# Key sums of two tiles at a time, a block of query projections moved, and another order at the start

## The chip, the cores and the metric

The program runs on one core of one Trainium2 chip. The engines that matter here are TensorE (PE: matmuls, and PEld: its weight loads), VectorE (DVE), ScalarE (ACT), GpSimd (POOL), and SyncE (SP), which issues most DMA transfers. Each engine takes its own instructions in order; semaphores hold an instruction until what it needs has been produced. The metric is the device time of one execution in microseconds (us), as the median of some runs.

## The reference

Linear attention, then a gated network, then a soft mixture of experts, in float32:

```python
def phi(x):                                   # q, k: (4 batches, 8 heads, 576, 64)
    proj = einsum('bhsd,df->bhsf', x, w_phi)  # 128 features
    proj = proj - max(abs(proj), axis=-1)
    return concatenate([exp(proj), exp(-proj)], axis=-1)
q_p, k_p = phi(q), phi(k)
kv = einsum('bhsf,bhsd->bhfd', k_p, v)
z  = sum(k_p, axis=2)
x  = einsum('bhsf,bhfd->bhsd', q_p, kv) / (einsum('bhsf,bhf->bhs', q_p, z) + 1e-6)
...
x = rms_norm(x) ; x = (silu(x @ w_gate) * (x @ w_val)) @ w_out     # 2304 tokens, 512 -> 1536 -> 512
...
d = softmax over tokens of (x @ phi) ; slots = d.T @ x ; experts ; c = softmax over slots
```

## The kernel before, in words

There are three stages. The first makes, for each of the four batches, the sums kv and z over its 576 keys, and the attention output of the first 384 query tokens (block 0). The second runs the gated network over six blocks of 384 tokens, with the queries of the later blocks turned into attention outputs in between. The third runs the experts. The change touches the first stage alone.

**Keys.** The 2304 keys are 18 tiles of 128. For each tile, class K does: `project` (L503, tile name P): 8 heads by 64-row matmuls, in two halves of four heads, the halves alternating; the two halves use different rows of the array and run side by side. `shift` for each half: on VectorE the largest absolute value (L507, `largest`) and the difference (L511, `less`). `exps` for each half: two exponentials on ScalarE (L524, L525) into a tile kp. `kv`: first `kv_of` for both halves (L548, kacc from kp and vt: each head's values as 64-column weights, two heads side by side), then `z_of` for both halves (L557, kacc from kp and small: a block of ones as 32-column weights, four heads side by side). They accumulate in PSUM over a batch. A batch is four and a half tiles, so tiles 4 and 13 are cut in two parts, and there are 20 parts. Where a batch ends, `Evac` copies its sums out (L570, L572) and three `fillers` transpose them (L585, kvt) and copy them into place (L594, L596). Each matmul in float32 leaves two records in the trace.

The loop over tiles i emits P and shift of tile i + 2, then the sums of tile i, then the exponentials of tile i + 2. P has two PSUM buffers, one for each half, so P of the next tile waits until `less` has read both halves of the one before. A pool named "misc" of three PSUM buffers is shared by the transposes of the sums and everything for block 0.

**Block 0.** Class Rows handles four pairs of heads. For each pair c and each of three 128-token pieces: `project` (L389, P from qraw; then L392 and L393 on VectorE), two half tiles later `turn` (L404 transposes, L406 exponentials), and once per pair `attend` (L449, o; L452 to L454). `scale` squares and normalizes rows (L465, L466 to L469), `out` transposes them back (L476, L477). Which half tile (2i or 2i + 1) each of these is emitted at is written out by hand in the list TURNED0: starts of the projections of the four pairs, then the four attend steps, then scale and out.

**Weights.** In the same stage nine pieces of the second stage's weights are loaded (L142) and converted on ScalarE and VectorE (L146, L148, L156, L158, L121, L124), one step each half tile from half tile 7.

**Order.** The instructions are emitted in this order, and a planner then orders each engine's instructions by its own estimate of when each is ready, with emission order as the priority. `placed(f, engines)` adds an edge so that the instructions that f emits on an engine stay behind the last one emitted there, and in their own order. WARM matmuls on zeros (L609) keep PE at work before the first keys have landed.

Of the kernel before, what the change touches and what calls it, by code (L numbers as in the profile page):

```python
# [7 lines left out]
F32 = mybir.dt.float32  # L8
F32R = mybir.dt.float32r
U32 = mybir.dt.uint32  # L10
AF = mybir.ActivationFunctionType
ALU = mybir.AluOpType
# [4 lines left out]
NB, NH, SEQ, HD, DF = 4, 8, 576, 64, 128  # L17
# [11 lines left out]
KCONV, MCONV = (3, 2), (2, 2)  # L29
NX = 4  # L30
CFIRST = 7
WARM = 3
NLEFT = 2
ELEFT = 4
CTURN = 4
# [1 line left out]
PADDED = [3, 3, 3, 6, 8, 8, 18, 13, 18]  # L37
PLAST = [2, 2, 2, 6, 9, 9, 15, 12, 15]
ADDED = [-6, -2, -1, 0, 2, 1, 2, 3, 4, 6, 6, 9, 8, 12, 10, 11, 13, 14, 13, 14, 16, 17, 18, 18, 21, 20, 24, 25, 28, 30]
TURNED0 = [2, 8, 14, 20, 12, 15, 20, 26, 28, 33]  # L40
TURNED1 = [0, 3, 10, 17, 6, 13, 20, 26, 27, 29, 31]


# [24 lines left out]
def tile_kernel(ctx: ExitStack, tc: tile.TileContext, q2T, qT, kT, v, wbd, wg, wv, wo, rmsg, phi, w1, w2, consts, out):  # L68
# [4 lines left out]
    def placed(f, *engines):  # L73

        traced = nc.cur_bb.bb.instructions
        start = len(traced)
        f()
        traced = nc.cur_bb.bb.instructions
        for engine in engines:
            last = next((i for i in reversed(traced[:start]) if i.engine == engine), None)  # L80
            for i in traced[start:]:
                if i.engine == engine:
                    if last is not None:
                        tc.add_manual_dep(i, last.name, nosync, reason="placed")
                    last = i
# [351 lines left out]
    class Rows(Turned):  # L437


        def attend(self, c):  # L440
            if c == 0:
                self.y = self.sp.tile([128, TPB, 4, 2, HD], F32, tag="y", name="y", bufs=1)
            e = [self.e.pop(2 * c), self.e.pop(2 * c + 1)]
            o = self.psum("o", [128, TPB, 2, HD + 1])
            for i in range(TPB):
                for b, r0, r1 in batch_parts(self.blk * TPB + i):
                    for hh in range(2):
                        for s in range(2):
                            PE.matmul(out=o[r0:r1, i, hh], lhsT=e[hh][:, s, 128 * i + r0:128 * i + r1],  # L449
                                      rhs=kvt[b][:, 2 * c + hh, s], start=s == 0, stop=s == 1, skip_group_check=True)  # L450
            rd = self.sp.tile([128, TPB, 2, 1], F32, tag="rd", name="rd", bufs=2)
            DVE.tensor_scalar(out=rd, in0=o[:, :, :, HD:HD + 1], scalar1=1e-6, scalar2=None, op0=ALU.add)  # L452
            DVE.reciprocal(out=rd, in_=rd)
            DVE.tensor_tensor(out=self.y[:, :, c], in0=o[:, :, :, 0:HD], in1=rd.to_broadcast([128, TPB, 2, HD]), op=ALU.mult)  # L454
            for b, t0, t1 in block_parts(self.blk):
                if c == 3 and self.blk * BLK + t1 == (b + 1) * SEQ and b + 2 < NB:
                    kvt[b + 2] = kvp.tile([128, NH, 2, HD + 1], F32, tag="kv", name=f"kv{b + 2}", bufs=2)
                    SP.dma_start(out=kvt[b + 2].rearrange("p h s d -> p (h s d)"), in_=kv_d[b + 2])

        def scale(self):  # L460
            sq = self.sp.tile([128, 2, 2, BLK], F32, tag="e", name="sq", bufs=self.bufs["e"]).rearrange("p a b t -> p (a b t)")
            ms = self.sp.tile([128, TPB], F32, tag="ms", name="ms", bufs=1)
            rows = [self.y[:, i].rearrange("p c h d -> p (c h d)") for i in range(TPB)]
            for i in range(TPB):
                ACT.activation(out=sq[:, DM * i:DM * i + DM], in_=rows[i], func=AF.Square, accum_out=ms[:, i:i + 1])  # L465
            DVE.tensor_scalar(out=ms, in0=ms, scalar1=1.0 / DM, scalar2=1e-6, op0=ALU.mult, op1=ALU.add)  # L466
            rsqrt(self.sp, ms)
            for i in range(TPB):
                DVE.tensor_scalar(out=rows[i], in0=rows[i], scalar1=ms[:, i:i + 1], scalar2=None, op0=ALU.mult)  # L469

        def out(self):
            xraw[self.blk] = xp.tile([128, 4, BLK], F32, tag="xraw", name="xraw", bufs=1)
            for c in range(4):
                tp = self.psum("yT", [128, TPB, 128])
                for i in range(TPB):
                    PE.transpose(out=tp[:, i], in_=self.y[:, i, c].rearrange("p h d -> p (h d)"), identity=ident)  # L476
                ACT.activation(out=xraw[self.blk][:, c].rearrange("p (i t) -> p i t", i=TPB), in_=tp, func=AF.Copy, scale=rms_sb[:, c:c + 1])  # L477

    with ExitStack() as pk:
        kx = pool(pk, "kx")  # L480
        sp = pool(pk, "spk")
        psk = pool(pk, "psk", PSUM)
        acc = {}

        class Front:

# [30 lines left out]
        class K(Front):  # L517
# [2 lines left out]
                SP.dma_start(out=self.vt, in_=v[self.i].rearrange("p (h d) -> p h d", h=NH))  # L520

            def exps(self, hf):
                kp = sp.tile([128, 4, 2, DF], F32, tag="kp", name="kp", bufs=6)
                ACT.activation(out=kp[:, :, 0], in_=self.pr[hf], func=AF.Exp)  # L524
                ACT.activation(out=kp[:, :, 1], in_=self.pr[hf], func=AF.Exp, scale=-1.0)  # L525
                self.e[hf] = kp

            def kv(self, part):

                for f in (self.kv_of, self.z_of):  # L530
                    for hf in range(2):
                        f(hf, part)

            def ends(self, part):
                b, r0, r1 = part
# [86 lines left out]
        for k in ks[0:2]:  # L622
            k.project()
            for hf in range(2):
                k.shift(hf)
                k.exps(hf)
        fillers = []
        q0 = Rows(sp, psk, 0, {"misc": 3, "raw": 2, "pr": 3, "e": 2})
# [3 lines left out]
        for i in range(TILES):  # L632
            k, kn = ks[i], ks[i + 2] if i + 2 < TILES else None
            if i + 4 < TILES:
                ks[i + 4].load()
            if i + 2 < TILES:
                ks[i + 2].load_v()
            parts = batch_parts(i)
            b = parts[0][0]
            ends = i * 128 + parts[0][2] == (b + 1) * SEQ  # L640

            def finish():
                ev = Evac(b)
                fillers.extend([lambda n=n: ev.turn(n) for n in range(3)])

            if len(parts) > 1:
                k.kv(parts[0])
                finish()
            if kn:
                kn.project()  # L650
                kn.shift(0)
                kn.shift(1)
            k.kv(parts[-1])
            for hf in range(2):
                if kn:
                    kn.exps(hf)
                n = 2 * i + hf - CFIRST
                if (n + 5) % 3 == 0 and 0 <= n + 5 and (n + 5) // 3 < NPRE:
                    placed(lambda: conv_load(sp, KCONV, sp), SP.engine)
                if n >= 0:  # L660
                    if n % 3:
                        conv_join()
                    else:
                        conv_parts()
                        conv_scale()
                if fillers:
                    fillers.pop(0)()
                for f in qsteps[2 * i + hf]:
                    f()
            if ends and len(parts) == 1:  # L670
                finish()
# [528 lines left out]
```

## Time and profile before

| | us |
|---|---|
| median of 3 runs | 704.33 (703.95 to 706.42) |
| profiled execution: time | 705.7 |
| profiled execution: span from first to last instruction | 703.9 |
| TensorE busy, share of the span | 689.4, 98% |
| VectorE busy | 468.5, 67% |
| ScalarE busy | 329.1, 47% |

The profile is of one execution. Busy time of an engine is the time in which one of its instructions ran; a matmul's end is modelled, so a busy PE need not be at its peak rate. "Idle before" names what ended an engine's idle time before an instruction. The granted clock of TensorE is a share of 2.4 GHz.

### The profile page before, as it was taken

What the parts mean: (1) busy time and instruction counts of PE and PEld (TensorE: products, weight loads), DVE (VectorE), ACT (ScalarE), POOL (GpSimd) and SP (SyncE); (2) the same over time, 40 slices, a digit from 0 to 9 for tenths busy, and PEclk for the clock granted to TensorE, in tenths of its full rate; (3) what the DMA queues carried; (4) which work ended last, traced back from release to release, by engine and by line L of the source; (5) the groups of instructions that cost most, each with busy time, mean ns of one, the idle gap of its engine ahead of it and who ended that gap; (6) DMA issues with size and microseconds to landing.
All of it is one profiled execution on the core that took longest, in us unless ns stands there. A gap on an engine that the chain in (4) does not pass through costs nothing.

```text
span 703.9 us, 11807 instructions
## 1 busy us (share of the span) xinstructions
PE 689.4 (98%) x4653; PEld 571.3 (81%) x4653; DVE 468.5 (67%) x915; ACT 329.1 (47%) x687; POOL 147.2 (21%) x74
## 2 busy tenths in 40 slices
PE   7999999999999999999999999999999999999995
PEld 4667766988889898998989989899897999898443
DVE  4798995888875596765857669776585753423313
ACT  4878885687745443344432554425443232112103
POOL 0000000000003355133651326523364200000100
PEclk9999999999999999999999999999999999999997
DMA  6755535434211001010000100001000085577898
GB/s 224 280 170 192 195 107 181 143 120 160 79 40 33 3 24 40 0 57 12 24 9 1 57 13 23 9 0 57 1 1 8 1 305 234 190 284 256 323 367 291
DMA packets 25143, 79.42 MB, mean 113 GB/s; under 512 B 2688, under 2 KB 13376, under 8 KB 18688
## 3 DMA queue, kind: packets, MB, share of 16 engines
q1 hardware_dynamic: 24720, 77.52, 31.4%
q10 hardware_dynamic: 368, 1.15, 0.5%
q8 instruction: 36, 0.59, 0.3%
q14 instruction: 19, 0.16, 0.1%
HBM read 71.99 MB, written 6.67 MB: 112 GB/s over the span
## 4 chain that ended last, share of the span: by engine, by line
PE 96%; DMA 1%; ACT 1%; DVE 1%; issue 0%; SPq 0%; ACTq 0%
PE pg L928 22%; PE pv L928 22%; PE acc L953 7%; PE acc L954 7%; PE acc L955 7%; PE kacc L548 5%; PE num L223 4%; PE P L503 3%; PE kacc L557 3%; PE y L1088 2%; PE y L1072 2%; PE o L449 2%; PE P L389 1%; DMA wraw<-in_wo_dram 1%; PE x2tp L738 1%; PE qP L315 1%
## 5 line engine op out<-in xcount | busy, mean ns | idle before, releaser
L928 PE MATMUL pv<-xnh,wv 128*128 128x384 f32 x576 | 117.1, 343 | 0.0
L928 PE MATMUL pg<-xnh,wg 128*128 128x384 f32 x576 | 115.1, 342 | 0.3 <-ACT xnh L121 0.3
L318 POOL PARTITION_ALL_REDUCE qe<-qe x32 | 51.9, 1634 | 297.1 <-ACT qe L317 287.9
L928 PEld LDWEIGHTS pg<-xnh,wg 128*128 128x128 f32 x576 | 102.5, 188 | 5.8 <-ACT xnh L121 0.7
L928 PEld LDWEIGHTS pv<-xnh,wv 128*128 128x128 f32 x576 | 101.7, 188 | 1.5 <-issue 1.3
L349 POOL PARTITION_ALL_REDUCE qe<-qe x32 | 82.7, 2631 | 85.8 <-DVE qe L348 56.3
L121 ACT CAST hh<-t 128x384 fp32r<-128x384 f32 x72 | 36.7, 509 | 115.2 <-PE acc L954 77.6
L953 PE MATMUL acc<-wo,hh 128*128 128x512 f32 x216 | 87.2, 404 | 0.0
L954 PE MATMUL acc<-wo,hh 128*128 128x512 f32 x216 | 86.1, 399 | 0.0
L955 PE MATMUL acc<-wo,hl 128*128 128x512 f32 x216 | 85.3, 395 | 0.0
L124 DVE TENSOR_TENSOR hl<-t,hh 128x384 fp32r<-128x384 f32 x72 | 40.1, 557 | 63.3 <-ACT hh L121 63.2
L936 DVE SCALAR_TENSOR_TENSOR t<-t,pg 128x384 f32<-128x384 f32 x72 | 39.8, 553 | 57.9 <-ACT t L935 57.7
L935 ACT ACTIVATE t<-pg 128x384 f32<-128x384 f32 x72 | 35.1, 487 | 73.1 <-PE pg L928 72.7
L928 PE MATMUL pg<-xnl,wg 128*128 128x384 f32 x288 | 65.0, 342 | 0.0
L928 PE MATMUL pv<-xnl,wv 128*128 128x384 f32 x288 | 62.4, 339 | 0.0
L940 DVE TENSOR_TENSOR t<-t,pv 128x384 f32<-128x384 f32 x72 | 39.6, 549 | 24.6 <-PE pv L928 23.6
L928 PEld LDWEIGHTS pg<-xnl,wg 128*128 128x128 f32 x288 | 51.9, 188 | 1.6 <-DVE xnl L124 0.9
L928 PEld LDWEIGHTS pv<-xnl,wv 128*128 128x128 f32 x288 | 51.7, 188 | 0.0
L955 PEld LDWEIGHTS acc<-wo,hl 128*128 128x128 f32 x216 | 40.6, 188 | 10.2 <-DVE hl L124 0.3
L953 PEld LDWEIGHTS acc<-wo,hh 128*128 128x128 f32 x216 | 40.8, 189 | 7.3 <-issue 0.3
L954 PEld LDWEIGHTS acc<-wo,hh 128*128 128x128 f32 x216 | 40.6, 188 | 6.3
L548 PE MATMUL kacc<-kp,vt 128*64 128x256 f32 (+1 forms) x320 | 41.2, 393 | 2.3 <-ACT kp L525 2.3
(207 smaller groups left out, 1051.7 us busy)
## 6 DMA issues: line engine op xcount, KB each, us to landing
eu<-in_w_dram SPq DMA_DIRECT2D x32, 1024.0 KB, 6.6
wraw<-in_wg_dram SPq DMA_DIRECT2D x6, 1024.0 KB, 4.9
wraw<-in_wv_dram SPq DMA_DIRECT2D x6, 1024.0 KB, 5.6
wraw<-in_wo_dram SPq DMA_DIRECT2D x6, 1024.0 KB, 5.5
qraw<-in_qT_dram SPq DMA_DIRECT2D x32, 192.0 KB, 2.4
vt<-in_v_dram SPq DMA_DIRECT2D x18, 256.0 KB, 3.2
out_dram<-ob SPq DMA_DIRECT2D x18, 256.0 KB, 3.0
raw<-in_kT_dram SPq DMA_DIRECT2D x17, 256.0 KB, 2.9
```

The source lines that it names most:

```text
L121: ACT.copy(out=hi, in_=src)
L124: (lo_eng or POOL).tensor_tensor(out=lo, in0=src, in1=hi.bitcast(F32), op=ALU.subtract)
L318: POOL.partition_all_reduce(e[:, 0], e[:, 1], channels=128, reduce_op=bass_isa.ReduceOp.absmax)
L349: POOL.partition_all_reduce(e[hh][:, 1], u, channels=128, reduce_op=bass_isa.ReduceOp.add)
L548: PE.matmul(out=kva[o0:o0 + 64, hh // 2], lhsT=self.vt[r0:r1, h], rhs=kp[r0:r1, hh].rearrange("p s f -> p (s f)"), start=first and hh < 2, ...
L928: PE.matmul(out=p, lhsT=w[:, a, c], rhs=x, start=n == 0, stop=n == 11)
L935: ACT.activation(out=t, in_=g, func=AF.Tanh, scale=0.5)
L936: DVE.scalar_tensor_tensor(out=t, in0=t, scalar=1.0, in1=g, op0=ALU.add, op1=ALU.mult)
L940: DVE.tensor_tensor(out=t, in0=t, in1=wide("v", m, xs), op=ALU.mult)
L953: PE.matmul(out=acc[i], lhsT=hh[:, s], rhs=w[:, 0], start=m == 0, stop=False)
L954: PE.matmul(out=acc[i], lhsT=hh[:, s], rhs=w[:, 1], start=False, stop=False)
L955: PE.matmul(out=acc[i], lhsT=hl[:, s], rhs=w[:, 0], start=False, stop=m == MF - 1)
```

## The change

The sums z of a part are no longer issued behind its key-value matmuls: the part is put in a list `zs`, and the list is worked off when it holds two parts or the part ends its batch. kp gets 8 buffers instead of 6. The number of warm-up matmuls rises from 3 to 4. For the first two tiles VectorE's instructions are placed in emission order (largest, less of one half, then of the other; the same for tile 1), and the projections of tiles 2, 3 and 4 are placed on PE. In TURNED0 the projections of pair 1 start at half tile 11 (8 before), those of pair 2 at 15 (14), and the attend steps of pairs 1 and 2 are at 17 and 21 (15 and 20). Block 0's attention output is kept in the tile xraw from the start, and transposed and written back in place, so its own tile y goes.

```diff
-WARM = 3
+WARM = 4
-TURNED0 = [2, 8, 14, 20, 12, 15, 20, 26, 28, 33]
+TURNED0 = [2, 11, 15, 20, 12, 17, 21, 26, 28, 33]
...
         def attend(self, c):
             if c == 0:
-                self.y = self.sp.tile([128, TPB, 4, 2, HD], F32, tag="y", name="y", bufs=1)
+                xraw[self.blk] = xp.tile([128, 4, BLK], F32, tag="xraw", name="xraw", bufs=1)
...
-            DVE.tensor_tensor(out=self.y[:, :, c], in0=o[:, :, :, 0:HD], ...)
+            DVE.tensor_tensor(out=xraw[self.blk][:, c].rearrange("p (i h d) -> p i h d", i=TPB, h=2), in0=o[:, :, :, 0:HD], ...)
...
-            rows = [self.y[:, i].rearrange("p c h d -> p (c h d)") for i in range(TPB)]
+            rows = [xraw[self.blk][:, :, 128 * i:128 * i + 128] for i in range(TPB)]
...
         def out(self):
-            xraw[self.blk] = xp.tile([128, 4, BLK], F32, tag="xraw", name="xraw", bufs=1)
...
-                    PE.transpose(out=tp[:, i], in_=self.y[:, i, c].rearrange("p h d -> p (h d)"), identity=ident)
+                    PE.transpose(out=tp[:, i], in_=xraw[self.blk][:, c, 128 * i:128 * i + 128], identity=ident)
...
-        acc = {}
+        acc, zs = {}, []
...
-                kp = sp.tile([128, 4, 2, DF], F32, tag="kp", name="kp", bufs=6)
+                kp = sp.tile([128, 4, 2, DF], F32, tag="kp", name="kp", bufs=8)
...
             def kv(self, part):
-                for f in (self.kv_of, self.z_of):
-                    for hf in range(2):
-                        f(hf, part)
+                for hf in range(2):
+                    self.kv_of(hf, part)
+                zs.append((self, part))
+                if len(zs) == 2 or self.ends(part)[1]:
+                    for k, p in zs:
+                        for hf in range(2):
+                            k.z_of(hf, p)
+                    zs.clear()
...
         for k in ks[0:2]:
             k.project()
             for hf in range(2):
-                k.shift(hf)
+                placed(lambda: k.shift(hf), DVE.engine)
                 k.exps(hf)
...
             if kn:
-                kn.project()
+                placed(kn.project, *[PE.engine] * (i < 3))
                 kn.shift(0)
                 kn.shift(1)
```

## Rows read from the trace of the kernel before

**Rows 1.** Page, busy time by engine: us, share of the span, instructions.

```profile
PE 689.4 (98%) x4653; PEld 571.3 (81%) x4653; DVE 468.5 (67%) x915; ACT 329.1 (47%) x687; POOL 147.2 (21%) x74
```

**Rows 2.** Windows by stage: length, busy time by engine, PE clock, DMA share, GB/s.

```profile
13.20:118.05 104.85, 103.20 (x1092) 68.50 (x1091) 89.22 (x155) 80.86 (x151) 0.00 (x0) 1.00 0.52 178
118.05:643.00 524.95, 524.81 (x2987) 469.61 (x2988) 354.06 (x699) 230.69 (x497) 144.26 (x68) 1.00 0.20 71
```

**Rows 3.** Windows in the beginning, same columns.

```profile
7.22:9.48 2.26, 0.00 (x1) 0.00 (x0) 2.26 (x5) 1.20 (x3) 0.00 (x0) 1.00 0.96 347
9.70:13.00 3.30, 3.30 (x12) 0.96 (x8) 1.54 (x3) 2.96 (x6) 0.00 (x0) 0.50 0.80 300
```

**Rows 4.** Timeline of the beginning: start, duration, engine, line, instruction, idle before.

```profile
1.18 2.77 PE L609 MATMUL idle<-still 128*32 128x256 f32 x6 [1.18 <-DVE small L606]
...
4.25 2.97 PE L503 MATMUL P<-wbd_f,raw 64*128 64x128 f32 x32 [0.30 <-DMA raw<-in_kT_dram]
...
6.36 1.29 DVE L507 TENSOR_REDUCE mx<-P 128x4 f32<-128x512 f32 x2 [1.70 <-PE P L503]
...
8.28 0.63 ACT L524 ACTIVATE kp<-pr 128x512 f32<-128x512 f32 x1 [3.62 <-DVE pr L511]
...
9.48 1.88 PE L548 MATMUL kacc<-kp,vt 128*64 128x256 f32 x8 [2.26 <-ACT kp L525]
...
13.21 1.17 PE L503 MATMUL P<-wbd_f,raw 64*128 64x128 f32 x16
...
14.41 1.29 DVE L507 TENSOR_REDUCE mx<-P 128x4 f32<-128x512 f32 x2 [3.17 <-PE P L503]
...
17.33 1.49 PE L503 MATMUL P<-wbd_f,raw 64*128 64x128 f32 x16
...
20.76 1.13 PE L389 MATMUL P<-wbd_f,qraw 128*128 128x256 f32 x4
```

**Rows 5.** Chain of work that ended last, tiles 15 and 16: start, time until the next.

```profile
95.99 0.22 PE kacc L557 x5
...
104.43 1.09 PE P L503 x16
105.52 1.88 PE kacc L548 x16
107.40 1.00 PE kacc L557 x16
```

**Rows 6.** Timeline around the wait in mid-stage.

```profile
36.99 1.19 ACT L146 ACTIVATE wt<-wraw 128x1024 f32<-128x1024 f32 x1 [0.74 <-DMA wraw<-in_wo_dram]
...
40.84 0.70 PE L389 MATMUL P<-wbd_f,qraw 128*128 128x256 f32 x2 [1.33 <-ACT kv L596]
```

**Rows 7.** Timeline: VectorE's last differences and PE's next projections.

```profile
70.12 1.28 DVE L511 TENSOR_TENSOR pr<-P,mx 128x512 f32<-128x512 f32 x2
...
71.88 1.16 PE L503 MATMUL P<-wbd_f,raw 64*128 64x128 f32 x16
...
82.75 1.28 DVE L511 TENSOR_TENSOR pr<-P,mx 128x512 f32<-128x512 f32 x2
...
84.97 1.16 PE L503 MATMUL P<-wbd_f,raw 64*128 64x128 f32 x16
```

**Rows 8.** Window over tiles 10 to 17, columns as before.

```profile
61.64:108.33 46.69, 46.69 (x510) 31.50 (x509) 45.30 (x82) 38.11 (x73) 0.00 (x0) 1.00 0.44 142
```

**Rows 9.** Timeline: two engines writing parts of one tile.

```profile
71.89 0.63 ACT L596 COPY kv<-kvt 128x256 f32<-128x256 f32 x2
...
72.44 0.75 DVE L594 COPY kv<-kvt 128x256 f32<-128x256 f32 x2
```

**Rows 10.** Lines by form, 0 to 118 us: busy us, mean ns, idle before.

```profile
L511 DVE TENSOR_TENSOR pr<-P,mx 128x512 f32<-128x512 f32 x36 | 23.2, 684 | 0.0
...
L392 DVE TENSOR_REDUCE qmx<-P 128x2 f32<-128x256 f32 x12 | 5.1, 422 | 1.3 <-PE P L389 1.2
...
L469 DVE TENSOR_SCALAR y<-y,ms 128x512 f32<-128x512 f32 x3 | 1.3, 482 | 0.0
```

More of the change, by code (lines that the diff above doesn't have):

```diff
@@ L453, in attend @@
             DVE.reciprocal(out=rd, in_=rd)
-            DVE.tensor_tensor(out=self.y[:, :, c], in0=o[:, :, :, 0:HD], in1=rd.to_broadcast([128, TPB, 2, HD]), op=ALU.mult)
+            DVE.tensor_tensor(out=xraw[self.blk][:, c].rearrange("p (i h d) -> p i h d", i=TPB, h=2), in0=o[:, :, :, 0:HD], in1=rd.to_broadcast([128, TPB, 2, HD]), op=ALU.mult)
             for b, t0, t1 in block_parts(self.blk):
@@ L462, in scale @@
             ms = self.sp.tile([128, TPB], F32, tag="ms", name="ms", bufs=1)
-            rows = [self.y[:, i].rearrange("p c h d -> p (c h d)") for i in range(TPB)]
+            rows = [xraw[self.blk][:, :, 128 * i:128 * i + 128] for i in range(TPB)]
             for i in range(TPB):
-                ACT.activation(out=sq[:, DM * i:DM * i + DM], in_=rows[i], func=AF.Square, accum_out=ms[:, i:i + 1])
+                ACT.activation(out=sq[:, DM * i:DM * i + DM].rearrange("p (c t) -> p c t", c=4), in_=rows[i], func=AF.Square, accum_out=ms[:, i:i + 1])
             DVE.tensor_scalar(out=ms, in0=ms, scalar1=1.0 / DM, scalar2=1e-6, op0=ALU.mult, op1=ALU.add)
```

## Prediction, made before the changed kernel was run

> **What bounds the kernel now.** I read the page's busy times first: TensorE (PE) is busy 98% of the span [rows 1]. Then the windows by stage: the first stage, after its beginning, runs from 13.20 to 118.05 us with PE busy 103.20 of 104.85 us, and the second is closed to within 0.2 us [rows 2]. So after the beginning the program is one string of PE work, and the change can gain only what PE idles, what it runs at a lower clock, or what it spends between kinds of matmul. Nothing in the diff touches the second or third stage; what the first stage gains moves the rest forward whole.
>
> Next the beginning. In the timeline, look at who waits for whom: PE projects tiles 0 and 1 (P, from 4.25), VectorE (DVE) takes maxima and differences from 6.36, ScalarE (ACT) starts exponentials at 8.28, and PE waits 2.26 us, to 9.48, for the first of them [rows 4]. The windows show PE empty from 7.22 to 9.48 and then a granted clock of 0.50, that is 1.2 of 2.4 GHz, over 9.70 to 13.00 [rows 3]. P of tile 2 comes only at 13.21, though its PSUM buffers were free when VectorE went idle at 11.24 (14.41 less 3.17) [rows 4].
>
> Last the two places where PE could lose time later: the one wait in mid-stage, 1.33 us before 40.84 for a copy on ACT [rows 6], and how closely VectorE follows PE. VectorE is busy 45.30 of 46.69 us between 61.64 and 108.33 [rows 8], with PE never waiting there: two engines near their limit side by side.
>
> **The change part by part.**
>
> *Feature sums two by two.* A tile costs PE a projection of 1.09 us, a key-value group of 1.88 and a sum group (z) of 1.00 [rows 5]. In z four matmuls run side by side; one round takes 0.22 (the row of the last five), and 16 records are four rounds, 0.86 (at 0.215). The other 0.14 is the change of array shape, paid on entering and leaving z. There are 20 parts of tiles (18 tiles, two cut by a batch's end). With sums held until two are there or the batch ends, each batch of five parts makes three z groups, not five: 12, not 20, so 8 times 0.14 = 1.1 us. Where tile 15 is followed by tile 16 with no projection between, two key-value groups also join; eight rounds of 0.215 are 1.72 of 1.88, so 0.16 more. Bounds: nothing, if the planner parts the joined groups again; 0.4 each if all idle time of the weight loads around a z went too. I take 0.14: it is counted from the group itself. One merge falls into the beginning (below); the other seven with the joined key-value groups give **1.1**. The two extra kp buffers only hold what waits; v tiles are released by the key-value matmuls as before, so SP's queue is not held longer.
>
> *The beginning.* The fourth warm-up matmul is two more records at the pace of the first six, at most 2.77 / 6 = 0.46 each [rows 4]: they end near 4.6 to 4.8, and P starts near 4.7, not 4.25. As the later rounds of P then run at the higher rate, its end for tile 0 moves less: VectorE starts near 6.6 (0.27 later; bounds 0, if the load lands later still, and 0.86). VectorE's eight instructions took 6.36 to 11.24, 0.61 each. Now they go in pairs, maximum then difference of one half, so the first half is ready after two, not three: 6.6 + 1.2, and ACT starts near 7.9 (8.28 before); PE follows 1.2 after ACT's start, as now [rows 4], near 9.1, and with P of tile 1 ending near 7.5 (7.22 before) it idles 1.6 us, not 2.26. VectorE is through with tile 1 near 11.5; P of tile 2 can start then, not at 13.21, if the planner puts it there: the new chain on PE keeps P after what precedes it in the program and its two halves interleaved. Tile 3's P took 1.42 to the next group (1.09 interleaved), 0.33 lost [rows 4, 5]. Adding up what PE must do from there: P2 to 12.7, key-values of tile 1 to 14.6, both z groups to 16.45, P3 to 17.55. Before, the same work was done at 20.76 [rows 4]. That is 3.2 us if the clock stays up. If it falls again, PE is at half speed to about 13 and the same sum ends at 18.55: 2.2 us. Which? After 2.26 us of idling it fell [rows 3]; after the 1.33 us before 40.84 [rows 6] the next groups are at full pace. 1.6 us is nearer to the second, but no row decides it. I take **2.7**; bounds 0.5 (only the VectorE order helps) and 3.4.
>
> *Three half tiles later.* At half tile 8 and 9 two projections of block 0 were due among the transposes of batch 0's key-value sums. All share three "misc" PSUM buffers; ACT, late because its weight scaling waited 0.74 us for a load, copied them out late, and the projection stood 1.33 us at the head of PE's queue [rows 6], with the next tile's P behind it. The projections now come at half tiles 11 to 13. The work is the same: per projection one matmul, two transposes and VectorE's reduction (0.42) [rows 10] and subtraction. Pair 2 moves one half tile, the attention steps of pairs 1 and 2 two and one. SP's load of pair 3 is issued three half tiles later, 7 half tiles ahead of its use. With only three transposes left, the misc buffers suffice: gain **1.33** (bounds 0, if the same wait comes later, and 1.33).
>
> *y in place of its own tile.* Rows of a token tile are now four runs of 128, not 512 in one run. The three scalings took 482 ns each [rows 10], on the way to the transposes. If strides cost, the nearest row above is a two-input instruction of the same 512 elements, 684: at most 0.6 us in all. I take 0: four instructions of 128 have the same elements, and key-value and sum groups of tiles 16 and 17 can stand in PE's queue meanwhile. The Trainium skill, "VectorE: DVE Perf Modes", section What auto-detection actually checks, ties the double rate to an even outermost dimension, which four runs keep; by it the term is 0 too, and no row here shows a strided one. ScalarE writes back into the tile that PE still transposes from; two engines do write parts of one tile at once here (ACT 71.89 to 72.52, VectorE from 72.44) [rows 9], so parts are tracked apart: 0.
>
> *What is late next.* A tile that gives up its z has 1.0 us less PE work before the next P, and that P needs VectorE's last difference. For tile 12's P there were 0.48 us to spare (71.40 to 71.88), for tile 14's 0.94 (84.03 to 84.97) [rows 7]. Both follow tiles that defer (9 and 11), and the moved attention step puts about 0.9 us of VectorE work before the first. So 0.3 to 1.1 us of waiting at the first, about 0.1 at the second, and up to 0.6 each at two others: 0.3 to 2.2; I take **1.0** lost, as the receiving tile gives nothing back while PE is the bound.
>
> Sum: 2.7 + 1.33 + 1.1 - 1.0 = 4.1 us. The profiled execution took 705.7 us with a span of 703.9; the sum makes it 701.6 and 699.8. It was 1.4 above the median of the runs, 704.33, which I forecast at **700.2**.
>
> **The rivals.**
> *The beginning gives little.* PE takes instructions in order, and the planner orders by its own times; it put single key-value and z matmuls ahead of P2 before. If it still does, only VectorE's new order helps, 0.5 of 2.7: 702.4. For it: the chain binds P to what precedes it, not what follows to P. Against: with paired halves everything is ready earlier.
> *The wait moves.* The moved projections meet attention steps and transposes for the same misc buffers where VectorE is 97% busy [rows 8]; then the 1.33 comes back, and VectorE's waits may reach their upper bound: 701.5 to 702.7. Against: PE was busy without a break from 61.64 to 108.33, through the same kind of steps [rows 8].
> *Pairs of sums save nothing.* If the 0.14 belongs to the matmuls themselves, or the planner parts them: 1.26 less gain, 701.5. Against it: 0.22 for a round of z.
> *Slower.* One mechanism: VectorE, not PE, sets the pace in every deferring tile. Then PE waits there up to the 1.0 us it no longer spends, and the sum work, put into the next tile, comes on top. With eight such tiles, and gains of 5.1 before waits, it decides from 0.64 us a tile; at 1.0 the loss is 8.0 and the time 707.2. Against it: the tiles in [rows 7] are the tightest of the deferring ones, and they have half a microsecond and more of the 1.0.
>
> **How the numbers follow.** A difference under 0.5%, 3.5 us, is about what cannot be told from no change. Forecast (698.9 to 701.3) 0.50; the wait moves 0.20; beginning gives little 0.15; sums save nothing 0.10; slower 0.05. Faster than 700.8 are most of the first case and the lower ends of the next three: 0.56. Slower than 707.9 lies only beyond the last case: 0.03. The rest, 0.41, is within. From 698.7 to 702.6 hold the first four but for tails; that leaves under 2 in 10 out.
>
> **What would show it.** Right: 12 z groups in the timeline, of 32 records and 1.86 us where joined; P of tile 2 near 11.6; no 0.50 clock, or a shorter spell; no PE wait for ACT's copy; second stage starting near 114.0, not 118.05. Wrong: new PE waits for VectorE before P in tiles 9 and 11, key-value matmuls standing ahead of P2, a wait for a misc buffer between 50 and 80 us, or PE waiting for the scaled rows before the last transposes.

## The result, and the profile after

The changed kernel takes **708.95 us** (median of 4 runs, 708.60 to 709.48), the kernel before on the same chip 704.53 (4 runs, 703.95 to 706.42). The ratio is 1.0059 with a 95% interval of 1.0038 to 1.0079: slower by some 4 us, where 700.2 was forecast. In some of the experiments below a part of the runs took 10 us or more longer than the others, for a reason that no run shows; ratios are of the shorter runs.

The profiled execution took 708.62 us with a span of 706.7 (before: 705.7 and 703.9), so the traces account for 2.9 of the 4.4 us; the profiled execution of before was one of its longer ones. First the page's busy times, as in [rows 1]:

```profile
PE 693.6 (98%) x4655; PEld 573.9 (81%) x4655; DVE 468.6 (66%) x915; ACT 329.4 (47%) x687; POOL 147.2 (21%) x74
```

PE has 4.2 us more busy time for two more records, those of the fourth warm-up matmul. The windows say where, with the columns of [rows 2]:

```profile
13.20:118.05 104.85, 104.83 (x1062) 69.07 (x1061) 88.14 (x152) 79.17 (x145) 0.00 (x0) 1.00 0.52 178
7.22:9.48 2.26, 0.47 (x10) 0.28 (x8) 2.19 (x5) 1.15 (x2) 0.00 (x0) 1.00 0.97 322
9.70:13.00 3.30, 3.30 (x27) 1.39 (x23) 2.35 (x4) 2.88 (x6) 0.00 (x0) 1.00 0.88 318
61.64:108.33 46.69, 46.69 (x482) 32.66 (x480) 42.75 (x74) 36.98 (x72) 0.00 (x0) 1.00 0.40 131
120.31:645.26 524.95, 524.80 (x2987) 469.45 (x2988) 354.06 (x699) 230.75 (x497) 144.25 (x68) 1.00 0.20 71
```

Several things that I had forecast are here. From 9.70 to 13.00 the granted clock is 1.00 where [rows 3] had 0.50, with 27 records done for 12. From 13.20 on PE is never idle: the wait of [rows 6] is gone, and the list of waits has for the rest of the first stage only this:

```profile
PE pg L932 <- ACT xnh L121: 0.3, 1, 0.3
```

The second stage is the same work in the same time [rows 2]. But it starts at 120.31, 2.26 us later than before. From 61.64 to 108.33 PE is busy all the time as in [rows 8], and gets through 482 records for 510. It is full and does less. VectorE, 45.30 us busy there before, has 42.75, more idle time than it had.

The timeline of PE's groups in the beginning (start, duration, records) shows how that can be:

```profile
4.73 2.87 PE L502 MATMUL P<-wbd_f,raw 64*128 64x128 f32 x32
9.39 1.08 PE L552 MATMUL kacc<-kp,vt 128*64 128x256 f32 x8 [1.79 <-ACT kp L524]
10.40 0.64 PE L561 MATMUL kacc<-kp,small 128*32 128x256 f32 x8
10.97 0.65 PE L552 MATMUL kacc<-kp,vt 128*64 128x256 f32 x2
11.55 0.49 PE L502 MATMUL P<-wbd_f,raw 64*128 64x128 f32 x2
11.96 1.08 PE L552 MATMUL kacc<-kp,vt 128*64 128x256 f32 x6
12.97 0.62 PE L561 MATMUL kacc<-kp,small 128*32 128x256 f32 x2
13.52 0.65 PE L552 MATMUL kacc<-kp,vt 128*64 128x256 f32 x2
14.10 1.16 PE L502 MATMUL P<-wbd_f,raw 64*128 64x128 f32 x14
...
18.05 0.48 PE L502 MATMUL P<-wbd_f,raw 64*128 64x128 f32 x2
18.46 0.62 PE L561 MATMUL kacc<-kp,small 128*32 128x256 f32 x2
19.01 1.16 PE L502 MATMUL P<-wbd_f,raw 64*128 64x128 f32 x14
20.10 0.63 PE L561 MATMUL kacc<-kp,small 128*32 128x256 f32 x6
20.66 1.13 PE L389 MATMUL P<-wbd_f,qraw 128*128 128x256 f32 x4
```

P of tile 2 starts at 11.55 (I had said 11.6), but with one matmul of its eight (a matmul has two records); the seven others follow at 14.10. Key-value (kv) and sum (z) groups are cut in the same way. The first query projection stands at 20.66, in [rows 4] at 20.76. The chain of waits (start, time until the next, records) shows the pieces behind it:

```profile
20.73 1.06 PE P L389 x4
21.79 1.44 PE kacc L552 x10
23.23 0.42 PE P L502 x2
23.64 0.58 PE kacc L552 x4
24.23 1.08 PE P L502 x14
25.31 0.58 PE kacc L552 x2
...
26.91 1.87 PE kacc L552 x14
28.78 1.42 PE P L502 x16
30.20 0.58 PE kacc L552 x2
30.77 1.86 PE kacc L561 x32
```

Set against a tile's chain in [rows 5]: a kv group is 1.88 whole and 1.44 + 0.58 + 0.58 = 2.60 as 10, 4 and 2 records; 1.87 + 0.58 = 2.45 as 14 and 2. P is 1.09 whole and 0.42 + 1.08 = 1.50 as 2 and 14. The P at 28.78 is not cut and still takes 1.42: its second half starts 0.33 us behind the first in the trace, where the halves of a P of 1.09 start together. The joined sums are 1.86 for 32 records, as forecast. Of whole and cut groups of kv, P and z the trace has 22, 17 and 11 from the first query projection to the second stage, before 18, 14 and 18.

### The profile page after: what moved, and what is told of

Same layout as the page of the kernel before. It is cut to its first block, busy times and chain, and to the rows that moved or that the text cites. A ratio compares the mean times of both kernels' runs of the same rounds, so it can differ in the third digit from the quotient of the medians.

```text
span 706.7 us, 11800 instructions
## 1 busy us (share of the span) xinstructions
PE 693.6 (98%) x4655; PEld 573.9 (81%) x4655; DVE 468.6 (66%) x915; ACT 329.4 (47%) x687; POOL 147.2 (21%) x74
## 4 chain that ended last, share of the span: by engine, by line
PE 94%; DMA 4%; DVE 1%; ACT 0%; issue 0%; SPq 0%
PE pg L932 22%; PE pv L932 22%; PE acc L957 7%; PE acc L958 7%; PE acc L959 7%; PE kacc L552 6%; PE num L223 4%; PE P L502 3%; PE kacc L561 3%; DMA eu<-in_w_dram 2%; PE P L389 2%; PE o L449 2%; DMA cT<-cT_d 1%; PE x2tp L742 1%; PE kvt L589 1%; PE T L404 1%
## 5 line engine op out<-in xcount | busy, mean ns | idle before, releaser
L959 PEld LDWEIGHTS acc<-wo,hl 128*128 128x128 f32 x216 | 40.6, 188 | 10.2 <-DVE hl L124 0.3
L552 PE MATMUL kacc<-kp,vt 128*64 128x256 f32 (+1 forms) x320 | 43.0, 386 | 1.8 <-ACT kp L524 1.8
```

What stands on the lines that cost most here:

```text
L552: PE.matmul(out=kva[o0:o0 + 64, hh // 2], lhsT=self.vt[r0:r1, h], rhs=kp[r0:r1, hh].rearrange("p s f -> p (s f)"), start=first and hh < 2, ...
L959: PE.matmul(out=acc[i], lhsT=hl[:, s], rhs=w[:, 0], start=False, stop=m == MF - 1)
```

## The experiments

Three theories stood after that. *Pieces*: the cuts cost PE's time by themselves. *VectorE*, or *late weights*: PE's stream only fills time in which VectorE, or ScalarE behind a weight's load, holds it back. *The planner cuts where PE would have waited*: the pieces are the price of waits. "Stretch" is the time from the first query projection to the second stage, 97.29 us before and 99.65 in the changed kernel.

**Holding PE's order, and each half alone.** The order is held by binding each of PE's instructions to the one ahead of it in the program, from tile 2, or from the first tile, on:

```
-        for i in range(TILES):
+        def tile_step(i):
...
+        for i in range(TILES):
+            placed(lambda: tile_step(i), *[PE.engine] * (i >= 2))
```

> The changed kernel, with PE's instructions held in emission order from tile 2 on, so that no projection or key-value group there is broken up; all else as changed. Theory 'pieces' (the changed kernel loses its gain because the planner cuts PE's groups into pieces, each costing a further change of array shape and matmuls that run alone): projections and key-value groups behind the first query projection take 53.2 us in the changed kernel and 49.1 before, for the same matmuls; most of that 4.1 comes back: 704.5 to 706. Theory 'VectorE' (the pieces only fill waits; VectorE sets the pace in tiles that defer their sums): PE now waits instead, 708 to 710, with waits for VectorE before projections in the trace.

> The same, with PE held in emission order from the first tile of the loop, so that the beginning too is in whole groups. Pieces: the beginning had 16 groups for 10.1 us of work; with 6 groups the first query projection comes at or before 20.7 us unless the long wait for tile 2's projection lowers the clock; 704 to 706. VectorE: as held_from_tile2, 708 to 710.

710.8 us, ratio 1.0077 (1.0061 to 1.0093), and 712.94, ratio 1.0106 (1.0089 to 1.0124): worse, and not the 704 to 706 that *pieces* alone would give. In the first the groups of the stretch are whole, and the timeline has waits in their place:

```profile
53.89 0.70 PE L389 MATMUL P<-wbd_f,qraw 128*128 128x256 f32 x2 [2.59 <-ACT e L406]
75.33 0.44 PE L404 MATMUL T<-cst,qpr 128*128 128x128 f32 x2 [1.23 <-ACT kv L600]
```

Behind the first of them the clock was 0.50 from 54.46 to 57.87. The misc buffers, which I had said suffice, do not: a query projection waits for ScalarE's exponentials out of a transposed one. So in this order of work something is paid either way.

The two halves alone, the kernel before with the lines of the change's diff for paired sums (with y's place and the kp buffers), and with its line TURNED0:

> The kernel before with the paired sums, the eight kp buffers and the output kept in xraw (which makes room for them), and nothing else. Pieces: 13 z groups, not 21, save about 1.2 us; one projection and one key-value group are newly cut, 0.4 and 0.6: 703.3 to 704.5. VectorE: tiles that defer their sums wait for VectorE, up to 1 us in each of eight: 706 to 712. Third theory (no cost in the change of array shape): 704.5 and no less PE time in z.

> The kernel before with the new list TURNED0 and nothing else. Pieces: the wait of 1.33 us in mid-stage goes, but four projections and one key-value group are newly cut, 0.4 to 0.6 each: 704.5 to 706. VectorE (moved work meets a VectorE that is already full): 706 or more, with PE waits for VectorE. The prediction's step: 703.2.

708.11 us, 1.0045 (1.0031 to 1.0060), and 709.02, 1.0050 (1.0032 to 1.0069). Both are slower, with stretches of 99.88 and 99.89. In the first the wait of [rows 6] is 2.39 us instead of 1.33, at 38.84, inside a cut P, and the clock falls behind it; one kv group is cut as well. The second has P in 18 groups for 14, one kv group cut, and a wait of 0.65.

**Are VectorE and ScalarE the bound?** First the nine weight loads of the first stage were left out, GpSimd setting the raw tiles:

```
+            if self.bufs is KCONV:
+                POOL.memset(self.raw.rearrange("p n w -> p (n w)").bitcast(F32), 1.0)
+                return
             SP.dma_start(out=self.raw.rearrange("p n w -> p (n w)"), in_=wsrc[nm][j].bitcast(U32))
```

> The kernel before, with the first stage's nine weight loads left out: GpSimd sets the raw tile to a constant, and the conversion works on that, so that the conversion's instructions stay on ScalarE and VectorE and no engine waits for a weight's transfer (the weights used later are therefore not the real ones). The question is asked of the pair, this one and the same edit of the changed kernel. Theory 'late weights' (ScalarE, held by a weight that has not landed, releases PSUM buffers late): this one is 0 to 2 us under the kernel before (it waits 1.9 us for weights), the changed one falls more, and the pair differs by less than 1.5 us. Theory 'VectorE full' (from 62 to 109 us VectorE's own work sets the pace): the pair still differs by 3 to 5 us. Theory 'pieces' (TensorE pays for cut groups): the pair still differs by 3 to 5 us.

> The changed kernel with the same edit: nine weight loads of the first stage left out, the raw tiles set by GpSimd. Theory 'late weights' (the trace of the changed kernel shows ScalarE waiting 6.6 us for weights in the first stage, against 1.9 before): 3 to 5 us under the changed kernel, some 704 us or less. Theories 'VectorE full' and 'pieces': within 1.5 us of the changed kernel, 707.5 to 710 us.

709.30, 1.0062 (1.0042 to 1.0083), and 710.02, 1.0077 (1.0056 to 1.0098). This is inconclusive: the planner drew a query projection to 9.8 us in both, ahead of its load, PE waited 3.0 and 2.3 us for it, and the clock was 0.50 for 10.2 and 3.4 us. The pair differs by 0.7 us, but with unequal spells at half clock, so it decides nothing.

Then the loads were kept and the conversion left out:

```
         def scale(self):
+            if self.bufs is KCONV:
+                return
...
+            if self.bufs is KCONV:
+                POOL.memset(u.bitcast(F32), 0.0)
+                return
             split(u[:, 0], u[:, 1], self.w, hi_eng=ACT, lo_eng=DVE)
```

> The kernel before with the weight loads of the first stage kept and their conversion left out (no scaling on ScalarE, no joining and splitting on VectorE; GpSimd clears the tiles that the second stage reads, so the weights are not the real ones). It frees some 4 to 5 us of VectorE and of ScalarE for each of nine weights. Theory 'VectorE full': the first stage becomes TensorE's, 1 to 4 us shorter than before, and the pair (this one and the same edit of the changed kernel) shows the change as it was costed on TensorE alone: the changed one 2.5 to 4.5 us faster. Theory 'late weights': the same, for nothing waits for a weight either. Theory 'pieces': the changed one is slower here too, by 2 to 5 us.

> The changed kernel with the same edit: weight loads kept, no conversion in the first stage. Theories 'VectorE full' and 'late weights': 2.5 to 4.5 us under the same edit of the kernel before. Theory 'pieces': 2 to 5 us over it.

703.34 us, 0.9986 (0.9971 to 1.0000), and 706.60, 1.0024 (1.0010 to 1.0037). The pair still differs by 3.3 us. Their windows over most of the first stage, before's first:

```profile
20.00:113.00 93.00, 92.98 (x993) 61.99 (x993) 55.03 (x117) 48.34 (x113) 0.00 (x0) 1.00 0.48 171
```

```profile
20.00:113.00 93.00, 92.98 (x967) 62.73 (x966) 56.61 (x120) 49.16 (x112) 0.00 (x0) 1.00 0.52 181
```

VectorE is busy 59 to 61% of that time and ScalarE 52 to 53%, PE waits for nothing in either, and the changed kernel does 26 records fewer. The theories of VectorE and of the weights fall, and with them the thought that PE's stream stretches to fill time: the stretches are 95.86 and 97.72 us.

**The price of a cut.** In the kernel before without conversion the next tile's P was put inside the kv group of 14 tiles, after four of its eight matmuls, or after one:

```
-                kn.project()
-                kn.shift(0)
-                kn.shift(1)
-            k.kv(parts[-1])
+            k.kv(parts[-1], following if kn and i >= 2 else None)
...
+                    if between and hh == 0:
+                        between()
```

(the lines of the second; `following` is the three calls, and PE's order is held, which by itself gives that kernel the order it has anyway).

> The kernel before without the weights' conversion in the first stage (as before_no_conversion: the weights are not the real ones), and with TensorE's instructions held in the program's order from tile 2 on, which is the order that kernel has anyway; the one thing changed is that in 14 tiles the next tile's projections stand in the middle of the kv matmuls and not ahead of them. The same matmuls, 14 more groups. Theory 'pieces' (each cut of a group costs TensorE's time): by the groups in the traces, two kv halves take 2.02 us for a whole's 1.88, and a P behind kv 1.42 for 1.09 behind z, so 0.47 us a cut: 6.6 us over before_no_conversion, 708.5 to 711 us. Theory 'VectorE or ScalarE sets the pace': they have nearly half their time free here, so no change from 703.3 us, plus or minus 1.

> As before_cut_no_conversion, with the same 14 cuts, the next tile's projections now between the first and the second of a tile's eight kv matmuls, which write the two column halves of the array. The even cut (four and four) cost 0.15 us a cut in the trace. Theory 'a cut between partners' (two matmuls on different halves of the array run side by side, and one that is left alone costs as much as two): 0.58 and 1.87 us for the two pieces against 1.88 whole, 0.57 a cut, 14 of them 8.0 us: TensorE's stretch from the first query projection to the second stage 103.5 to 104.5 us where before_no_conversion has 95.9, and 711 to 713 us. Theory 'any cut costs the same': as the even cut, 98.6 us in that stretch and 706.5 to 708.5.

The even cut: ratio 1.0031 (1.0012 to 1.0049), stretch 98.58, of which kv 35.88 against 33.78: 0.15 us a cut, a third of what I expected, because P behind a kv piece of eight still took 1.09. The odd cut: 713.22 us (711 to 713 expected), 1.0108 (1.0093 to 1.0124), stretch 103.80, of which kv 41.74: 0.57 us a cut, as expected. The chains, the even one first:

```profile
21.59 1.01 PE kacc L557 x8
22.60 1.09 PE P L510 x16
23.70 1.01 PE kacc L557 x8
```

```profile
21.79 0.58 PE kacc L556 x2
22.36 1.09 PE P L510 x16
23.46 1.87 PE kacc L556 x14
```

Read the two chains together with the pieces of the changed kernel: kv takes 0.58 for 2 and for 4 records, 1.01 for 8, 1.44 for 10, 1.87 for 14, 1.88 for 16. Time goes up by pairs. Each kv matmul writes one column half of the array (128*64 in the rows), and neighbours write different halves. The Trainium skill, "TensorE: Matmul & The Clock Gate", section Part 3: Packing small matmuls, says that matmuls on different tile positions of the array run concurrently; the trace agrees, one kv matmul and two take the same 0.58. A cut between partners makes each run alone, 0.57; a cut between pairs costs only the extra change of shape, 0.15. For z, four column quarters, 2, 6 and 8 records take 0.55 to 0.57, so a cut inside four costs 0.54; for P, two row halves, 2 and 14 cost 0.41.

**Whole groups without the conversion.**

> The changed kernel without the weights' conversion (as after_no_conversion), and with TensorE held in the program's order from tile 2 on: 95 groups where after_no_conversion has 101, 14 cut pieces where that has 25. Theory 'pieces': with VectorE and ScalarE half free nothing has to be waited for, so the cut groups' 2.5 to 3 us come back: 703 to 704.5 us against 706.6. Theory 'the planner cut groups only where TensorE would have waited': what is saved in pieces is paid in waits, and it stays within 1 us of 706.6 or above it.

> The kernel before without the weights' conversion (not the real weights), with the sums paired and TensorE held in the program's order: the merged sums alone, with no cut added and nothing to wait for. Theory 'pieces': seven merges at 0.14 us, TensorE's stretch 94.7 to 95.2 us against 95.86 of before_no_conversion, and the time 1 to 1.5 us under its 703.3. Rival (a merged sum delays the rows of sums that the next stage of the tile wants, and TensorE waits): the stretch 95.9 us or more.

The changed kernel, held: the times, 708.6 to 720.2 us, don't answer; its trace has a stretch of 97.20 against 97.72, kv and P 1.9 us less and the waits and transposes 1.4 more. So even with VectorE and ScalarE half free, three quarters of what the changed order's cuts cost come back as waits. The sums paired and nothing else, held: 704.18 us, 0.9983 (0.9969 to 0.9997); stretch 95.48 against 95.86, a miss of the 94.7 to 95.2 expected, for it has a wait of 0.36 us for ScalarE's copy that the other has not; z takes 17.32 against 18.01. The merged sums do save on PE, 0.7 us for seven; as a time of the kernel that can't be told from nothing.

**Looking for a version that keeps the gains.** The paired sums with the order held, and then the second pair of projections one or two half tiles later, and the whole change held with its two half tiles' query work on either side of kv:

```
-TURNED0 = [2, 8, 14, 20, 12, 15, 20, 26, 28, 33]
+TURNED0 = [2, 9, 14, 20, 12, 15, 20, 26, 28, 33]
```

> The kernel before with the sums paired (and the y tile's place and the buffers that go with it) and TensorE held in the program's order from tile 2 on; beginning and query projections as before. 90 groups of TensorE's matmuls with 6 cut pieces (before: 100 and 7; sums paired without holding: 10 pieces). Theory 'pieces': 7 merged sums at 0.14 us are 1 us less, and no cut pays it back: 702 to 704.5 us, unless the wait of a query projection on ScalarE's copy, 1.3 us before and 2.4 with the pairs, stays at 2.4 and takes the clock with it: then 705 to 708. Theory 'VectorE full': no faster than before, 704 to 706.

> pairs_held (707.4 us, with a wait of 2.2 us of a query projection for ScalarE's copy out of a transposed kv tile, behind which the clock fell for 3.4 us) with block 0's second pair of query projections one half tile later, so that the two transposes ahead of it stand together. Theory 'pieces and that one wait': without it 2.3 us of waiting and 1.6 us of half clock go, 702 to 704 us. Rival (the wait moves to the next taker of a PSUM buffer, as it did when the change was held whole): 705 to 709, with a wait of over 1 us for ScalarE or VectorE between 45 and 60 us.

> The same with the second pair of query projections two half tiles later. Theory 'pieces and that one wait': 702 to 704 us. Rival (the wait moves): 705 to 709.

> The whole change with TensorE held in the program's order from tile 2 on, and with the first half tile's query work and transposes put ahead of the kv matmuls and the second's behind them, so that the two don't stand together. 95 groups, 11 cut pieces, of which 9 stand in the first two tiles. Theory 'pieces and waits' (held as it was, the change lost 5 us in waits behind work that stood bunched together): spreading takes most of those waits, 702 to 706 us. Theory 'VectorE full': 707 us or more, with TensorE waiting for VectorE in the tiles of the second half.

707.43 us, 1.0030 (1.0014 to 1.0047): the wait for ScalarE's copy was 2.17 us, and the clock fell behind it, as the windows show:

```profile
36.10:38.30 2.20, 0.48 (x2) 0.30 (x2) 1.19 (x4) 2.20 (x7) 0.00 (x0) 1.00 0.09 31
38.50:41.90 3.40, 3.40 (x25) 2.61 (x26) 3.24 (x6) 1.35 (x2) 0.00 (x0) 0.50 0.15 12
```

One half tile later, 704.56, 0.9996 (0.9981 to 1.0011), two later 705.40, 1.0001 (0.9987 to 1.0014): the wait for ScalarE's copy shrank to 0.8 in the first and is gone in the second, which waits 0.3 for ScalarE's exponentials instead; no clock fell, but a wait of 0.9 us for ScalarE came before the last transposes. Their second stages start at 115.56 and 116.06, 2.0 to 2.5 us ahead of before's profiled execution, which had a spell at half clock that theirs had not. No version is shown to be faster than the kernel before. Spread out, 714.14 us, 1.0120 (1.0099 to 1.0141), with nine waits in the stretch: the guess was wrong.

**The beginning.** The kernel before with the diff's three edits of the beginning (WARM and the two calls of placed), and the whole change without the second of these calls:

```
-                placed(kn.project, *[PE.engine] * (i < 3))
+                kn.project()
```

> The kernel before with the three edits of the beginning alone (a fourth warm-up matmul, VectorE's two instructions of a half in pairs, the projections of tiles 2 to 4 held behind what stands ahead of them). The planner makes 108 groups of it, 22 of them cut pieces (before 100 and 7). The prediction's first term said 2.7 us faster, 701.8. Theory 'pieces between partners' (0.57 us a cut kv, 0.54 a cut z, 0.41 a cut P, where partners are parted): the beginning's clock comes back, but the first query projection stands at 20.0 us or later, and the cut groups of tiles 2 to 4 behind it cost some 1.5 to 2 us more: 705 to 707.5.

> The whole change but the holding of the projections of tiles 2 to 4. 97 groups of TensorE's matmuls and 20 cut pieces for 103 and 29; the beginning's cuts are even ones now (P four and four, kv four, two, two, three). From the pieces' durations in the traces: the beginning's groups 9.4 us for 11.3, and the tiles behind the first query projection two cut kv tiles and a cut P less, 2.0 us. Theory 'pieces between partners': 3 to 4 us under the changed kernel, 704.5 to 706. Rival (the cuts fill waits that were there anyway): 707.5 to 709.5.

The beginning alone: 708.49 us, 1.0038 (1.0023 to 1.0052), above the 705 to 707.5 that I gave it. Its first query projection is at 19.23, 1.5 us ahead of before (0.97 of that stands ahead of the first kv, where the projections of tiles 0 and 1 took 2.06 us in this execution and 2.97 in that of before), but its stretch is 99.89: cuts in tiles 2 to 4, and P of another tile cut at a wait of 1.7 us for the same copy as in [rows 6]. The change without the held projections: 706.56, 1.0019 (1.0005 to 1.0033), 2.4 us back, or 2.8 by the two ratios; the first query projection at 19.66, the stretch 98.30. In the two traces the stretch gives 1.35 of it and the groups from the first kv to the first query projection 0.15 (11.12 for 11.27); 0.84 is again the projections of tiles 0 and 1, 2.06 us for 2.87 with the same instructions. Its timeline shows the groups behind the beginning whole again:

```profile
20.73 1.16 PE L502 MATMUL P<-wbd_f,raw 64*128 64x128 f32 x16
21.82 1.95 PE L552 MATMUL kacc<-kp,vt 128*64 128x256 f32 x16
...
27.68 1.93 PE L561 MATMUL kacc<-kp,small 128*32 128x256 f32 x32
```

I had expected 3 to 4 us. The planner now put four P matmuls of one row half together, and eight records took 1.08, as long as sixteen of both halves: pieces that I had counted as even had no partners at all.

Whether the edits of the beginning keep the clock up is another matter. The kernel with the paired sums alone has three warm-up matmuls and VectorE's old order, and PE waits 2.26 us before the first kv as in [rows 4]. Yet no half clock followed:

```profile
8.95 1.08 PE L552 MATMUL kacc<-kp,vt 128*64 128x256 f32 x8 [2.26 <-ACT kp L524]
...
18.40 1.13 PE L389 MATMUL P<-wbd_f,qraw 128*128 128x256 f32 x4
```

The same eight records took 1.88 in [rows 4]. Three of the held kernels with paired sums (without the conversion, and with the second pair of projections at half tiles 8 and 9) show the same. Without the edits of the beginning, then, the clock fell in some executions (before, the two cut kernels, the moved projections alone) and not in others, and with four warm-up matmuls it fell too, behind a wait of 4.04 us in the held changed kernel without conversion.

## Why the prediction was wrong

*Feature sums two by two, 1.1.* Right in kind, 0.7 in the stretch: joined groups take 1.86 as forecast, but 2.00, no less than apart, in the two cases that join sums of 64 rows with sums of 128; the two kv groups joined take 3.60 for 3.76, the 0.16 of the sum. The trace has 16 z groups and not 12, for in the beginning z was cut, not joined.

*The beginning, 2.7.* Part of the mechanism came: VectorE's pairs, PE 0.5 us less idle before the first kv, P of tile 2 begun at 11.55. The clock was at 1.00 as well, but that this came of the edits is not shown, for the paired sums alone kept it at 1.00 with the beginning as before; as far as the runs go it was luck. The step that failed is "Adding up what PE must do from there": it added whole groups, 17.55, and real ones ended at 20.66. What the clock was worth shows in the kernel before without conversion, whose clock did not fall (its beginning has none of the edits): the groups that before ran from 9.48 to 20.76 [rows 3, 4], 11.28 us, take 9.68 there. So 1.6 came back with the clock, and the changed kernel, from 9.39 to 20.66, spends the same 11.27: its pieces ate all of it. The 0.57 gained ahead of 9.39 pays the fourth warm-up matmul, 0.48. The rival "the beginning gives little" had its place right (the chain binds P to what precedes it, not what follows to P) and its price wrong.

*Three half tiles later, 1.33.* The wait went, and the transposes of the kv sums take 6.01 us for 6.08: with the wait, the 1.40 of the sum below. But "with only three transposes left, the misc buffers suffice" failed: the projections moved to where the attention steps are, and there the planner put two of them and one of their transposes inside P and kv groups (2 and 14, 6 and 10, 2 and 14 records), or, held, PE waits 2.59 us for ScalarE.

*y in place of its own tile, 0.* Right: VectorE's three scalings take 478 to 483 ns [rows 10].

*What is late next, 1.0.* I priced lateness as a wait of PE for VectorE, and there is none. What turned the sign is a term that the sum puts at nothing: cut groups. In the stretch kv takes 36.06 us for 33.78 and P 17.16 for 15.33, 4.1 us, more than the waits I feared; 0.66 of it are two P groups that are whole but have their halves 0.33 apart. The cuts come of all three edits, not of late sums alone. Alone, the paired sums cut one P and one kv group of the stretch, the moved projections four and one, the beginning's edits two and two. And without the hold on the projections of tiles 2 to 4 the changed kernel's kv takes 34.84 and its P 16.67, so 1.7 of the 4.1 us is the price of that hold. Why the planner cut at each place is not shown; that work was late there is my reading. With 0.35 more for the query projections and their transposes, less the 1.40 and 0.69 of the terms above, the stretch is 2.4 us longer; 97.29 to 99.65 is what was measured. The rival "slower" had the time nearly right, 707.2, and the mechanism wrong: with VectorE and ScalarE half free the loss stays.

What the conversion-free pair shows is the pieces' price at work; that PE would have waited instead, for most of it, if nothing was cut is shown by the held kernels. So the cuts are dear but not simply a mistake: this order of projections, with three misc buffers, has to pay one or the other. Not settled: the remaining 1.5 us between the medians and the two profiled executions. The spell at half clock in the profiled execution of before is worth about as much, 1.6, but no execution of before without it was profiled with its conversion.

## What to carry to other kernels

Small matmuls that share the array are priced by the group: before costing an edit that lets a planner or a chain reorder TensorE, ask whether partners stay neighbours, and count the groups of the new order, not the matmuls. A full TensorE is no proof that it does useful work; compare the records done in equal windows. A merge saves one change of shape, 0.14 us here, and a cut between partners costs three or four times that, 0.41 to 0.57, so an edit that saves merges must be shown to add no cuts.

## What the runs showed of the hardware that was not expected

A matmul cut from its partner costs what the pair costs: 0.58 us for one or two kv matmuls, 1.08 for four P matmuls of one row half or eight of both. The cost is invisible as waiting: the trace shows PE busy throughout. And the length of PE's last wait did not tell whether the clock would fall. Waits of 2.17, 2.39 and 2.59 us in mid-stage were each followed by 3.4 us of records at a granted clock of 0.50 (1.2 of 2.4 GHz), while behind waits of 1.33 [rows 6], 1.61 (order held from the first tile) and 1.71 us (the beginning alone) it stayed at 1.00. But it fell behind a wait of 1.74 us with one of 0.19 after it (order held from the first tile, 0.50 from 28.44), and behind one of 1.26 with 0.18 after it (spread out, 0.50 from 41.68):

```profile
27.66 0.46 PE L502 MATMUL P<-wbd_f,raw 64*128 64x128 f32 x2 [1.74 <-issue]
28.30 1.92 PE L502 MATMUL P<-wbd_f,raw 64*128 64x128 f32 x14 [0.19 <-DVE pr L510]
```

```profile
40.81 0.46 PE L502 MATMUL P<-wbd_f,raw 64*128 64x128 f32 x2 [1.26 <-issue]
41.45 1.84 PE L502 MATMUL P<-wbd_f,raw 64*128 64x128 f32 x14 [0.18 <-DVE pr L510]
```

In the beginning a wait of 2.26 us was followed by 0.50 in the kernel before and by 1.00 in the kernel with the paired sums alone.
